# A third copy of q and k in DRAM: stored from SBUF at once, or copied later inside DRAM

## The chip, the cores and the metric

The kernel runs on one core of a Trainium2 chip. The metric is the device time in microseconds (us) of one execution, the median over several runs. The core has a matrix engine (PE, with a separate row PEld for loading weights), a vector engine (DVE), a scalar engine (ACT), a general engine (POOL), and a queue engine (SP) that issues every DMA of this kernel. The DMAs share 16 DMA engines.

## The reference

Attention over a sliding window and a dense GELU block read the same x, and a gate mixes them per row:

```python
def _A_ref(x, wqkv, wo):                 # B, S, D = 1, 2048, 512; H = 32; Dh = 16; W = 256
    qkv = (x @ wqkv).reshape(B, S, 3, H, Dh).transpose(2, 0, 3, 1, 4)
    q, k, v = qkv[0], qkv[1], qkv[2]
    scores = einsum("bhqd,bhkd->bhqk", q, k) * (Dh ** -0.5)
    mask = (idx[:, None] - idx[None, :] >= 0) & (idx[:, None] - idx[None, :] < W)
    p = softmax(where(mask, scores, -1e9))
    o = einsum("bhqk,bhkd->bhqd", p, v)
    return o.transpose(0, 2, 1, 3).reshape(B, S, D) @ wo
def _B_ref(x, w1, b1, w2, b2):           # F = 1792
    return gelu(x @ w1 + b1) @ w2 + b2
g = sigmoid((x * gate_w).sum(-1, keepdims=True))
return g * _A_ref(...) + (1 - g) * _B_ref(...)
```

Everything is float32.

## The kernel before

The matrix products are made of three passes over numbers that are split into a high part (rounded) and a low part (the rest): high times high, high times low, low times high. Lines 127, 128 and 129 (`mm3`) are these three passes.

The 2048 rows of x are cut into four tiles of 512 rows (t = 0 to 3). The PE's main stream is written by a generator, `dense`: first `qkv` for the four tiles (stage "qk", the first 146 us of the trace), then eight turns of the dense block (`mlp`, each with a stage "u" for the first product and a stage "y" for the second), then the output product (`final`). The attention is woven into that stream by the main loop over u. Its 32 heads form eight groups g of four heads, and each group has 16 key blocks of 128 rows, so u runs over 128 steps, with a lead of 12 steps for the pass that finds the row maxima (`att_max`, PE line 541, tile sm). The scores proper are `att_exp` (PE line 585, tile st, exponential on ACT in line 607), and the product with v is `att_pvs` (line 629).

q and k pass through DRAM. `qkv_qk` computes, for one tile t, 128 of q's columns (j = 0 to 3) or of k's (j = 4 to 7), and `qk_out` splits the result into a high and a low part, tile `qke`, and stores it into SQ[t] or SK[t]. There each row of a head has three slots: two for the two parts, and a third that repeats the high part, so that one matrix product over 48 rows of a head covers all three passes. The store is two DMAs: line 348 writes the two parts (512 KB) and line 349 writes the repeated part (256 KB), from the same tile in SBUF. Over the whole kernel these are 32 DMAs of each kind. Index i, the number of the 128 columns, runs from 0 to 3; the groups g = 0 to 3 read i = 0 and 1, the groups 4 to 7 read i = 2 and 3.

The loads for the attention are `load_kd` (line 509) and `load_qd` (lines 501, 496, 498) for the maxima, `load_ks` (the same three lines, tile ks) and `load_qs` (line 520) for the scores; `att_load_v` (line 526) brings v. In one group each of them comes once for every tile t. Their buffers have two slots, so a load waits until the PE has done with the block before the last.

The order of all instructions on PE, DVE, ACT, POOL and SP is written out when the kernel is built: `after` puts a step on a list with a due time in an assumed time, `tick` lets that time pass, and `need` draws a step forward when its result is wanted. On the chip, each engine goes through its own order, and an instruction that waits holds up all behind it. This holds for SP too. Its DMAs take eight completion counters in turn, so that a DMA is issued only when the one eight places before it has landed.

Weights of the dense block come through `load_now` (line 189, tile raw_w), are rounded by ACT (`split`, line 197, tile w) and completed by DVE (line 201).

Of the kernel before, what the change touches and what calls it, by code (L numbers as in the profile page):

```python
# [9 lines left out]
F32 = mybir.dt.float32  # L10
# [7 lines left out]
S, D, F, H, DH, W = 2048, 512, 1792, 32, 16, 256  # L18
T = 512
NT = S // T  # L20
NB = T // 128
NC = D // 128
# [10 lines left out]
def gated_mix(ctx: ExitStack, tc: tile.TileContext, x, wqkv, wo, w1, b1, w2, b2, gate_w, out):  # L33
    nc = tc.nc
# [6 lines left out]
    dr = ctx.enter_context(tc.tile_pool(name="dr", bufs=1, space=DRAM))  # L41
# [4 lines left out]
    def f32(ap):  # L46
        return ap.bitcast(F32)
# [9 lines left out]
    nc.gpsimd.memset(idle, 0.0)  # L57


    SQ = [dr.tile([H // NC, 16, 3, NC, T], F32, name=f"SQ{t}") for t in range(NT)]  # L60
    SK = [dr.tile([H // NC, 16, 3, NC, T], F32, name=f"SK{t}") for t in range(NT)]
    SV = [dr.tile([128, NB, 2, H // 2 * 17], F32, name=f"SV{t}") for t in range(NT)]
    XT = [dr.tile([NC, 128, 2, T], F32, name=f"XT{t}") for t in range(NT)]
    OT = [dr.tile([NC, 128, T], F32, name=f"OT{t}") for t in range(NT)]
# [47 lines left out]
    def halves(v):  # L112

        return v.rearrange("p (a c) -> p a c", a=2)
# [17 lines left out]
    now, todo, done = [0.0, 0], [], set()  # L132

    def after(ns, fn, *args):
        now[1] += 1
        heapq.heappush(todo, (now[0] + ns, now[1], fn, args))

    def step_todo():
        due, _, fn, args = heapq.heappop(todo)
        keep, now[0] = now[0], due  # L140
        fn(*args)
        now[0] = max(keep, due)

    def tick(ns):
        now[0] += ns
        while todo and todo[0][0] <= now[0]:
            step_todo()

    def need(*keys):
        for key in keys:  # L150
            while key not in done:
                step_todo()
# [103 lines left out]
        v = qd[:, i // 2, i % 2]  # L256
        nc.scalar.activation(v, nil.broadcast_to([128, 2 * T]), AF.Copy)

    xts, xrs = {}, {}

    def load_xr(t, bs=range(NB)):
        for b in bs:
# [69 lines left out]

    def qk_out(t, j, p):

        dst, i = (SQ[t], j) if j < NC else (SK[t], j - NC)
        e = sb.tile([128, 2, T], F32R, tag="h", bufs=7, name=f"qke{t}_{j}")

        h = 1 if j < NC else 0

        def hi():  # L340
            nc.scalar.activation(halves(e[:, h]), p, AF.Copy)  # L341

        def lo():
            nc.vector.tensor_sub(halves(e[:, 1 - h]), p, halves(f32(e[:, h])))  # L344

        def store():
            to = dst[:, :, :, i].rearrange("h d s c -> (h d) s c")
            nc.sync.dma_start(to[:, 0:2], f32(e))
            nc.sync.dma_start(to[:, 2], f32(e[:, h]))
            done.add(("qk", t, j))  # L350
        after(100, hi), after(700, lo), after(700 + HOLDQ, store)

# [109 lines left out]
                gate(t + 1)  # L462


    vts, Ms, pts = {}, {}, {}

    def slot(g_, c):
        return (g_ * NT + c) % 2

    def heads(st, g_):  # L470

        return st[2 * (g_ % 4):2 * (g_ % 4) + 2, :, :, 2 * (g_ // 4):2 * (g_ // 4) + 2]

    def ready(t, g_, k):
        need(*[("qk", t, k * NC + 2 * (g_ // 4) + a) for a in range(2)])

    def part(st, g_, s):

        return heads(st, g_)[s].rearrange("d u a c -> (d u) (a c)")

    def load_ks(g_, c):


        ready(c, g_, 1)
        n = 2 * NB
        put_pairs([f32(ks[64 * s + 4:64 * s + 52, slot(g_, c)]) for s in range(2)], SK[c], g_)

    def put_pairs(to, st, g_):

        n = 2 * NB  # L490
        for s in range(2):
            v = to[s].rearrange("r a x -> r (a x)")
            src = part(st, g_, s)
            if s:
                mid = v[:, 192:192 + 256 * (n - 1)].rearrange("r (n x) -> r n x", x=256)[:, :, 0:128]
                nc.sync.dma_start(mid, src[:, 64:64 + 128 * (n - 1)].rearrange("r (n x) -> r n x", x=128))
                ends = v.rearrange("r (n j) -> r n j", j=64)[:, 0:4 * n:4 * n - 1]
                nc.sync.dma_start(ends, src.rearrange("r (n j) -> r n j", j=64)[:, 0:2 * n:2 * n - 1])
            else:
                v = v.rearrange("r (n x) -> r n x", x=256)[:, :, 64:192]  # L500
                nc.sync.dma_start(v, src.rearrange("r (n x) -> r n x", x=128))

    def load_kd(g_, c):
        for t in range(max(c - 1, 0), c + 1):
            ready(t, g_, 1)
            k0 = 0 if t == c else T - W
            at = W if t == c else 0
            src = heads(SK[t], g_)[:, :, :, :, k0:].rearrange("s d u a c -> (s d u) a c")
            nc.sync.dma_start(f32(kd[0:96, slot(g_, c), :, at:at + T - k0]), src)

    def load_qd(g_, c):
        ready(c, g_, 0)
        put_pairs([f32(qd[48 * s:48 * s + 48, slot(g_, c)]) for s in range(2)], SQ[c], g_)

    def load_qs(g_, c):
        ready(c, g_, 0)
        need(("v", NT - 2, NB - 1))
        for s in range(2):
            v = f32(qs[64 * s + 4:64 * s + 52, :, c * T:(c + 1) * T])
            nc.sync.dma_start(v, part(SQ[c], g_, s).rearrange("r (a c) -> r a c", a=2))  # L520

    def att_load_v(g_, c):
        need(*[("v", c, b) for b in range(NB)])
        vt = vbuf[:, c % 2]
        dst = vt[:, 0:NB * 68].rearrange("p (j c) -> p j c", c=34)
        nc.sync.dma_start(dst, SV[c].rearrange("p j s c -> p (j s) c")[:, :, 34 * g_:34 * g_ + 34])
        vts[g_, c] = vt

    def att_max(g_, b, i):

        if b % RB == 0 and (g_, b // RB) not in Ms:
            Ms[g_, b // RB] = sb.tile([128, 2 * RB, 2], F32, tag="M", bufs=2, name=f"M{g_}_{b}")
        M = Ms[g_, b // RB]
        hb, pr = divmod(i, 2)
        c, n = b // NB, slot(g_, b // NB)
        j = 2 * (b % NB) + hb
        w = min(64 * (2 * b + hb + 1), W + 64)
        k1 = 64 * (j + 1) + W
        p = ps.tile([128, 320], F32, tag="sm", bufs=3, name=f"sm{g_}_{b}_{i}")
        v = pairs(p[:, :w])  # L540
        nc.tensor.matmul(v, qd[0:96, n, pr, 128 * j:128 * (j + 1)], two(kd[0:96, n, pr, k1 - w:k1]),  # L541
                         start=True, stop=True)

        def red():
            nc.vector.tensor_tensor_reduce(v, v, two(mask[:, 320 - w:320]), 1.0, -3e38,  # L545
                                           ALU.add, ALU.max, M[:, 2 * (b % RB) + hb, pr:pr + 1])
            done.add(("max", g_, b, i))
        tick(w / 2.4 + 13)
        after(100, red)
# [399 lines left out]
    def fill(ns):  # L949

        owed[0] += ns
        while owed[0] > 0:
            c = next(run)
            if c is None:
                owed[0] = -1e9
            else:
                owed[0] -= c
                tick(c)
# [7 lines left out]
    for u in range(-LEAD, NU):  # L966
        m = u + LEAD
        gm, bm = divmod(m, NKB)
        step = STEP if u >= 0 else STEP0
        for i in range(4):  # L970
            if i == 1 and m % NB == 0 and NB <= m < NU - NB:
                load_kd(*divmod(m // NB + 1, NT)), load_qd(*divmod(m // NB + 1, NT))
            if i % 2 == 0:
                pair = (i, i + 1) if stage[0] != "u" else (i,)
            elif len(pair) == 2:
                continue
            else:
                pair = (i,)
            for op, i in [(op, k) for k in pair for op in ORDER[:3]] + [("f", k) for k in pair]:
                if op == "s" and u >= 0:  # L980
                    att_exp(u // NKB, u % NKB, i)
                if op == "m" and m < NU:
                    att_max(gm, bm, i ^ XOR)
                if op == "p" and i == PVAT and 1 <= u <= NU - LEAD:
                    att_pvs(u - 1)
                if op == "f":
                    fill(step / 4)
        if m < NU and bm % RB == RB - 1:
            after(900, att_rows, gm, bm // RB)
        if m % NB == QAT % NB and QAT <= m < QAT + NKB:  # L990
            load_qs(0, (m - QAT) // NB)
        if u > NU - LEAD:
            att_pvs(u - 1)
        if u % NB == 0 and NB <= u < NU - NB:
            load_ks(*divmod(u // NB + 1, NT))
        if u % NB == 2 and NB < u < NU - 3 * NB:
            load_qs(*divmod(u // NB + 3, NT))
        if u % NB == 0 and u >= 0:
            att_load_v(*divmod(u // NB, NT))
        if u - NU + NKB == YAT:  # L1000
            for k in range(6):
                after(1500 + YGAP * k, load_y, *divmod(k, 2))
    for n, c in enumerate(run):
        tick(c or 0)
        if n == HELD:
            att_pvs(NU - 1)
# [33 lines left out]
AHEAD = 9e3  # L1040
STEP0 = 2750.0
PVAT = 2
HELD = 2
YAT = 5
YGAP = 2500
# [21 lines left out]
```

## Time and profile before

| what | value |
|---|---|
| time, median of 3 runs | 717.82 us (714.51 to 720.12) |
| the profiled execution's own time | 720.44 us |
| its span, first to last instruction | 718.6 us |
| mean granted clock of the PE | 0.994 |
| PE busy | 696.9 us (97% of the span) |
| DVE busy | 514.2 us (72%) |
| ACT busy | 420.0 us (58%) |
| POOL busy | 363.5 us (51%) |
| DMA | 172.09 MB, mean 239 GB/s |
| stores of the repeated part, line 349 | 32 of 256 KB |

The views give times in us from the span's start. In a view of windows the engines stand with the time they were busy in the window and the number of instructions, then the PE's granted clock as a share of full speed, the mean busy share of the DMA engines (it can come out a little above 1) and the rate at which they moved data. In a timeline a row has its start, its length, engine, line and operation, and in brackets the idle time before it and what ended it. A row of SPq is the issue of a DMA; the transfer itself comes after. In the chain of waits a DMA's piece reaches from its issue to its landing. Lines "A <- B: 5.1, 8, 1.0" say that A waited for B for 5.1 us in all, 8 times, at most 1.0 us.

### The profile page before, as it was taken

Reading aid. Unit: us, or ns where it says so; the run is one execution under the profiler, and the core shown is the slowest. Engines: PE = TensorE matmul, PEld = TensorE weight load, DVE = VectorE, ACT = ScalarE, POOL = GpSimd, SP = SyncE. Lnnn points to the kernel's source line nnn. Section 1 sums busy time; section 2 is a strip of 40 time slices with the busy share of each in tenths; the row PEclk is TensorE's granted clock in tenths of the full one; section 3 lists DMA queues with packets and bytes.
Section 4 is the critical chain, followed back from the end, with each engine's and each line's share of the span. In section 5 each row is a group of like instructions: output and inputs, shape, how many; then the busy total and the mean of one; then the engine's idle time right before and its main releaser. Section 6 shows DMA issues by size and latency. Waiting matters only on the chain.

```text
span 718.6 us, 17501 instructions
## 1 busy us (share of the span) xinstructions
PE 696.9 (97%) x6129; PEld 599.8 (83%) x6129; DVE 514.2 (72%) x1561; ACT 420.0 (58%) x972; POOL 363.5 (51%) x852
## 2 busy tenths in 40 slices
PE   9999999988999999999999999999999999999998
PEld 7888888776888888888888878888888888868877
DVE  3732425778868977987898789868877986875552
ACT  4434532348546944964696469548845953885451
POOL 4200000548766875786687657757765785620000
PEclk9999999999999999999999999999999999999999
DMA  8989898998998698799776989997799899578573
GB/s 296 355 264 408 286 400 252 286 329 199 276 261 194 149 261 218 192 221 273 187 186 162 243 219 234 236 273 175 187 267 231 211 263 248 137 214 224 191 254 118
DMA packets 179255, 172.09 MB, mean 239 GB/s; under 512 B 56672, under 2 KB 122976, under 8 KB 179168
## 3 DMA queue, kind: packets, MB, share of 16 engines
q1 hardware_dynamic: 179168, 170.97, 85.9%
q8 instruction: 49, 0.80, 0.5%
q14 instruction: 38, 0.31, 0.2%
HBM read 108.53 MB, written 62.39 MB: 238 GB/s over the span
## 4 chain that ended last, share of the span: by engine, by line
PE 76%; DMA 9%; DVE 6%; ACT 6%; issue 1%; SPq 1%; POOL 1%; DVEq 0%; ACTq 0%
PE sm L541 8%; PE st L585 7%; PE pv_sm L629 7%; PE y L127 6%; PE y L129 6%; PE y L128 6%; PE u L127 5%; PE u L129 4%; PE u L128 4%; PE qk L127 3%; PE qk L129 3%; PE qk L128 3%; DMA qd<-SQ 2%; DVE sm L545 2%; DMA raw_w<-in_B_w_dram 2%; PE pv_st L629 2%
## 5 line engine op out<-in xcount | busy, mean ns | idle before, releaser
L545 DVE CUSTOM_DVE_ANT_1 sm<-sm,mask 128x320 f32<-128x320 f32 (+4 forms) x512 | 233.0, 485 | 71.1 <-PE sm L541 66.0
L601 POOL TENSOR_SCALAR_AFFINE_SELECT pt<-pt 64x256 f32<-64x256 f32 (+1 forms) x538 | 215.0, 420 | 102.4 <-ACT pt L607 91.8
L607 ACT ACTIVATE pt<-st 128x320 f32<-128x320 f32 (+4 forms) x512 | 195.4, 422 | 118.2 <-PE st L585 117.4
L541 PE MATMUL sm<-kd,qd 96*128 96x320 f32 (+4 forms) x512 | 148.6, 304 | 8.4 <-DVE M L545 5.1
L585 PE MATMUL st<-qs,ks 128*128 128x320 f32 (+4 forms) x512 | 148.0, 300 | 2.6 <-ACT pt L607 2.5
L567 POOL CAST qs<-tt 4x256 fp32r<-4x256 f32 x256 | 120.2, 470 | 42.7 <-DVE tt L560 31.4
L541 PEld LDWEIGHTS sm<-kd,qd 96*128 96x128 f32 x512 | 97.4, 190 | 28.0 <-DVE M L545 11.7
L585 PEld LDWEIGHTS st<-qs,ks 128*128 128x128 f32 x512 | 98.1, 192 | 14.6 <-ACT pt L607 4.5
L127 PE MATMUL y<-w,h 128*128 128x512 f32 x224 | 85.1, 380 | 0.6 <-DVE sqh L746 0.6
L129 PE MATMUL y<-w,h 128*128 128x512 f32 x224 | 84.9, 379 | 0.0
L128 PE MATMUL y<-w,h 128*128 128x512 f32 x224 | 84.8, 379 | 0.0
L127 PE MATMUL u<-mx,w 128*128 128x512 f32 x196 | 77.4, 395 | 1.2 <-DVE sqh L746 1.2
L129 PE MATMUL u<-mx,w 128*128 128x512 f32 x196 | 74.8, 382 | 0.0
L128 PE MATMUL u<-mx,w 128*128 128x512 f32 x196 | 74.7, 381 | 0.0
L629 PE MATMUL pv_sm<-pt,vbuf 64*32 64x320 f32 (+4 forms) x1408 | 73.2, 346 | 0.2 <-POOL pt L601 0.2
L629 PE MATMUL pv_st<-pt,vbuf 64*32 64x320 f32 (+4 forms) x1408 | 72.9, 346 | 0.0
L545 DVE DVE_READ_ACCUMULATOR2_ANT M<- 128x1 f32 x512 | 71.4, 139 | 0.0
L629 PEld LDWEIGHTS pv_sm<-pt,vbuf 64*32 64x32 f32 x1408 | 49.3, 106 | 20.2 <-issue 2.0
L344 DVE TENSOR_TENSOR qke<-qk,qke 128x512 fp32r<-128x512 f32 x32 | 22.1, 689 | 43.2 <-ACT qke L341 33.9
L341 ACT ACTIVATE qke<-qk 128x512 fp32r<-128x512 f32 x32 | 19.1, 597 | 49.9 <-PE qk L129 34.8
L129 PEld LDWEIGHTS y<-w,h 128*128 128x128 f32 x224 | 42.2, 189 | 6.1
L127 PEld LDWEIGHTS y<-w,h 128*128 128x128 f32 x224 | 42.5, 190 | 3.2 <-DVE sqh L746 0.8
(148 smaller groups left out, 1292.0 us busy)
## 6 DMA issues: line engine op xcount, KB each, us to landing
kd<-SK SPq DMA_DIRECT2D x32, 384.0 KB
qs<-SQ SPq DMA_DIRECT2D x64, 192.0 KB
mx<-XT SPq DMA_DIRECT2D x24, 512.0 KB
SQ<-qke SPq DMA_DIRECT2D x16, 512.0 KB
SK<-qke SPq DMA_DIRECT2D x16, 512.0 KB
ND<-nd SPq DMA_DIRECT2D x32, 256.0 KB
raw_w<-in_B_w_dram SPq DMA_DIRECT2D x28, 256.0 KB
qd<-SQ SPq DMA_DIRECT2D x32, 192.0 KB
```

The source lines that it names most:

```text
L127: nc.tensor.matmul(p, lh, rh, start=first, stop=False)
L128: nc.tensor.matmul(p, lh, rl, start=False, stop=False)
L129: nc.tensor.matmul(p, ll, rh, start=False, stop=last)
L341: nc.scalar.activation(halves(e[:, h]), p, AF.Copy)
L344: nc.vector.tensor_sub(halves(e[:, 1 - h]), p, halves(f32(e[:, h])))
L541: nc.tensor.matmul(v, qd[0:96, n, pr, 128 * j:128 * (j + 1)], two(kd[0:96, n, pr, k1 - w:k1]), start=True, stop=True)
L545: nc.vector.tensor_tensor_reduce(v, v, two(mask[:, 320 - w:320]), 1.0, -3e38, ALU.add, ALU.max, M[:, 2 * (b % RB) + hb, pr:pr + 1])
L567: nc.gpsimd.tensor_copy(dst, src.unsqueeze(1).broadcast_to([4, 2, RB, 32]))
L585: nc.tensor.matmul(pairs(p[:, :w]), ks[:, slot(g_, kb // NB), pr, at:at + 128], two(qs[:, pr, k0:k0 + w]), start=True, stop=True)
L601: nc.gpsimd.affine_select(out=v, in_=v, pattern=[[0, v.shape[1]], [1 - 2 * e, 64]], compare_op=ALU.is_ge, fill=0.0, base=-e, channel_multi ...
L607: nc.scalar.activation(halves(pt[:, hf, pr, :w]), sorted_(p[:, :w]), AF.Exp, scale=SCALE)
L629: nc.tensor.matmul(pv[r // 64][32 * i:32 * i + 32, q - c * T:e - c * T], vts[g_, b // NB][r:r + 64, v:v + 32], rhs(r), start=start, stop=s ...
```

## The change

SQ[t] and SK[t] are each cut into two DRAM tensors, one with i = 0 and 1 and one with i = 2 and 3. For i = 0 and 1 nothing else changes. For i = 2 and 3 `qk_out` stores the two parts as before but not the repeated one. It notes the copy that is to be made, from the slot of the high part to the third slot, in a list `twice`. The main loop takes one copy from the list at each odd u from 17 to 47, and `repeat` issues it as a DMA from DRAM to DRAM on SP. The loads of the groups 4 to 7 need the copy, where they needed the store. There are 16 such copies of 256 KB, in place of 16 of the 32 stores.

```diff
-    SQ = [dr.tile([H // NC, 16, 3, NC, T], F32, name=f"SQ{t}") for t in range(NT)]
-    SK = [dr.tile([H // NC, 16, 3, NC, T], F32, name=f"SK{t}") for t in range(NT)]
+    SQ = [[dr.tile([H // NC, 16, 3, 2, T], F32, name=f"SQ{t}_{i}") for i in range(2)] for t in range(NT)]
+    SK = [[dr.tile([H // NC, 16, 3, 2, T], F32, name=f"SK{t}_{i}") for i in range(2)] for t in range(NT)]
...
     def qk_out(t, j, p):
-        dst, i = (SQ[t], j) if j < NC else (SK[t], j - NC)
+        i = j % NC
+        dst = (SQ, SK)[j // NC][t][i // 2]
...
         def store():
-            to = dst[:, :, :, i].rearrange("h d s c -> (h d) s c")
+            to = dst[:, :, :, i % 2].rearrange("h d s c -> (h d) s c")
             nc.sync.dma_start(to[:, 0:2], f32(e))
-            nc.sync.dma_start(to[:, 2], f32(e[:, h]))
+            if i < 2:
+                nc.sync.dma_start(to[:, 2], f32(e[:, h]))
+            else:
+                twice.append((t, j, to[:, 2], to[:, h]))
             done.add(("qk", t, j))
...
+    def repeat():
+
+        t, j, to, by = twice.pop(0)
+        nc.sync.dma_start(to, by)
+        done.add(("twice", t, j))
...
     def heads(st, g_):
-        return st[2 * (g_ % 4):2 * (g_ % 4) + 2, :, :, 2 * (g_ // 4):2 * (g_ // 4) + 2]
+        return st[g_ // 4][2 * (g_ % 4):2 * (g_ % 4) + 2]
 
     def ready(t, g_, k):
-        need(*[("qk", t, k * NC + 2 * (g_ // 4) + a) for a in range(2)])
+        need(*[(("qk", "twice")[g_ // 4], t, k * NC + 2 * (g_ // 4) + a) for a in range(2)])
...
+        if COPY[0] <= u < COPY[1] and u % 2 == 1 and twice:
+            repeat()
...
+COPY = (17, 49)
```

PE, DVE, ACT and POOL keep the same instructions in the same order. Only SP's order changes, at two kinds of places. The first is where the stores were; this is the last tile (t = 3), around the end of stage qk. In the rows, SQ_82 and SK_86 are tile 3's q and k, qke_2 and qke_6 stand for i = 2, qke_3 and qke_7 for i = 3, and kd and qd are the loads for tile 3 of group 0. SP before:

```order
L189 DMA raw_w_1507<-in_B_w_dram 128x4x128
L348 DMA SQ_82<-qke_2_1502 128x2x512
L349 DMA SQ_82<-qke_2_1502 128x512
L189 DMA raw_w_1507<-in_B_w_dram 128x512
L348 DMA SK_86<-qke_6_1537 128x2x512
L349 DMA SK_86<-qke_6_1537 128x512
L509 DMA kd<-SK_85 96x2x256
L509 DMA kd<-SK_86 96x2x512
L501 DMA qd<-SQ_82 48x8x128
```

SP in the changed kernel, at the same place (line 348 has become 349, 509 is 519 and 501 is 511; SQ_1_86 and SK_1_94 are the second tensors of tile 3, SK_0_93 and SQ_0_85 the first):

```order
L189 DMA raw_w_1503<-in_B_w_dram 128x4x128
L349 DMA SQ_1_86<-qke_2_1498 128x2x512
L189 DMA raw_w_1503<-in_B_w_dram 128x512
L349 DMA SK_1_94<-qke_6_1532 128x2x512
L519 DMA kd<-SK_0_91 96x2x256
L519 DMA kd<-SK_0_93 96x2x512
L511 DMA qd<-SQ_0_85 48x8x128
```

The two stores of the repeated part that stood ahead of the loads kd and qd are gone; everything else stands as it stood. The next two, for i = 3, go in the same way a few rows further on.

The second kind of place is where the copies are. SP before, at u = 17 to 20 (ND is a store of the attention's result, qs and kd and qd are loads of group 1 and 2):

```order
L526 DMA vbuf<-SV_87 128x8x34
L657 DMA ND_0_111<-nd_3_2812 128x512
L520 DMA qs<-SQ_82 48x2x512 x2
L509 DMA kd<-SK_83 96x2x256
L509 DMA kd<-SK_84 96x2x512
L501 DMA qd<-SQ_80 48x8x128
```

SP in the changed kernel (line 472 is the copy; 536, 667, 530 and 519 are the lines 526, 657, 520 and 509 of before):

```order
L536 DMA vbuf<-SV_95 128x8x34
L667 DMA ND_0_119<-nd_3_2804 128x512
L472 DMA SQ_1_80<-SQ_1_80 128x512
L530 DMA qs<-SQ_0_85 48x2x512 x2
L472 DMA SK_1_88<-SK_1_88 128x512
L519 DMA kd<-SK_0_87 96x2x256
L519 DMA kd<-SK_0_89 96x2x512
L511 DMA qd<-SQ_0_81 48x8x128
```

One copy stands ahead of the load qs and one ahead of the loads kd and qd, and so it goes on, two copies for every four steps of u, to the last copy, which stands directly ahead of the first load of group 4.

More of the change, by code (lines that the diff above doesn't have):

```diff
@@ L257, in clear_q @@
         nc.scalar.activation(v, nil.broadcast_to([128, 2 * T]), AF.Copy)
-    xts, xrs = {}, {}
+    xts, xrs, twice = {}, {}, []
     def load_xr(t, bs=range(NB)):
```

## The prediction, made before the changed kernel was run

> **What bounds the kernel now.** I read the page's first part, then who the PE waits for, and then the stretches in which it waits.
>
> ```profile
> PE 696.9 (97%) x6129; PEld 599.8 (83%) x6129; DVE 514.2 (72%) x1561; ACT 420.0 (58%) x972; POOL 363.5 (51%) x852
> PE sm L541 <- DVE M L545: 5.1, 8, 1.0
> PE st L585 <- ACT pt L607: 2.5, 3, 1.5
> PE sm L541 <- DMA qd<-SQ: 2.1, 1, 2.1
> 0.00:140.00 140.00, 137.63 (x692) 120.10 (x693) 63.44 (x161) 57.35 (x143) 23.95 (x60) 1.00 0.94 321
> 140.00:175.00 35.00, 29.14 (x138) 24.45 (x137) 27.83 (x83) 20.56 (x41) 20.78 (x34) 0.95 0.95 262
> 220.00:350.00 130.00, 130.00 (x1333) 113.56 (x1333) 107.65 (x360) 84.94 (x200) 89.73 (x218) 1.00 0.84 212
> ```
>
> The PE is the bound: of a span of 718.6 us it is idle for 718.6 - 696.9 = 21.7 us, and no change to DMAs can win more than that and what the clock loses. The windows (length, busy us of PE, PEld, DVE, ACT, POOL, then clock, DMA share, GB/s) say where. Up to 140 us, the stage in which the stores are made, the PE is idle for only 2.4 us, although the DMA engines are busy to 0.94. From 140 to 175 us, where the attention and the first turn of the dense block begin, it is idle for 35 - 29.14 = 5.9 us, more than a quarter of all its idle time in a twentieth of the span. From 220 to 350 us, where the copies will go, it is not idle at all, and the DMA engines have 16% left.
>
> So two questions decide: how far the DMAs end the waits between 140 and 175 us, and whether the copies fit into 220 to 350 us.
>
> **The place that waits for DMAs.** First the PE's two longest waits there (its timeline), with ACT's row that belongs to the second, then the clock in windows of 5 us, then the chain of waits in this stretch, then SP's issues of the four stores that go.
>
> ```profile
> 157.42 0.37 PE L541 MATMUL sm<-kd,qd 96*128 96x320 f32 x1 [2.13 <-DMA qd<-SQ]
> 171.70 0.40 PE L585 MATMUL st<-qs,ks 128*128 128x320 f32 x1 [1.51 <-ACT pt L607]
> 170.69 0.63 ACT L197 ACTIVATE w<-raw_w 128x512 fp32r<-128x512 f32 x1 [2.03 <-DMA raw_w<-in_B_w_dram]
> 155.00:160.00 5.00, 2.87 (x11) 2.34 (x10) 2.62 (x9) 2.01 (x5) 1.27 (x1) 0.77 1.04 365
> 160.00:165.00 5.00, 5.00 (x26) 4.46 (x25) 4.84 (x15) 4.75 (x11) 3.22 (x7) 0.89 1.02 274
> 165.00:170.00 5.00, 5.00 (x29) 4.47 (x27) 4.24 (x13) 3.62 (x9) 4.61 (x9) 1.00 1.15 204
> 170.00:175.00 5.00, 2.62 (x12) 1.59 (x11) 3.65 (x7) 4.09 (x9) 4.70 (x8) 1.00 0.58 144
> ```
>
> ```profile
> 149.27 7.59 DMA qd<-SQ
> ...
> 157.36 6.04 DMA SK<-qke
> 163.41 0.02 issue
> 163.42 7.24 DMA raw_w<-in_B_w_dram
> 170.67 0.02 issue
> 170.69 0.64 ACT w L197
> 171.33 0.02 issue
> 171.35 1.74 DVE w L201
> ```
>
> ```profile
> 144.12 0.47 SPq L349 DMA_DIRECT2D SQ<-qke  x1
> 146.70 0.54 SPq L349 DMA_DIRECT2D SK<-qke  x1
> 153.57 0.33 SPq L349 DMA_DIRECT2D SQ<-qke  x1
> 157.36 0.47 SPq L349 DMA_DIRECT2D SK<-qke  x1
> ```
>
> The first wait, 2.13 us, ends with the load qd of tile 3, which was issued at 149.27 and took 7.59 us, in a stretch where the DMA engines' share stands at 1.04. Two of the stores that go were issued 5.2 and 2.6 us before it. Right after this wait the granted clock falls (0.77 and 0.89 in the two windows), which costs 0.23 x 5 + 0.11 x 5 = 1.7 us of PE time. The second wait, 1.51 us, is put down to ACT, but ACT itself had stood for 2.03 us for a weight, raw_w, with the exponential behind it in its queue. The chain shows why that weight was late: it was issued at 163.42, as soon as the store SK<-qke that SP had issued at 157.36 had landed, and this is one of the four stores that go (SP lets only eight DMAs be under way). Both waits hang on one stream of DMAs that is full from 145 to 170 us; at 170 to 175 us its share falls to 0.58, so the backlog is gone there.
>
> **What the removal is worth.** The price of a store comes from the stretch that is made of such stores and little else (87 to 103 us), a row of the view of DMAs:
>
> ```profile
> DMA packets 2933, 6.37 MB, mean 398 GB/s; under 512 B 244, under 2 KB 436, under 8 KB 2932
> ```
>
> 262,144 bytes at 398 GB/s are 0.66 us of all engines. At the mean rate of 140 to 175 us, 262 GB/s (windows above), it would be 1.0 us. I take 0.66, since that row is of the same operation. Step by step:
>
> 1. Twelve of the 16 stores belong to tiles 0 to 2, before 103 us. They free 12 x 0.66 = 7.9 us of DMA time, but the PE idles 2.4 us in all before 140 us, and these rows say for what:
>
> ```profile
> PE warm0.0_180 L386 <- POOL idle L57: 1.2, 1, 1.2
> PE xp L280 <- DMA xr<-in_A_x_dram: 0.4, 1, 0.4
> 132.02 0.48 PE L127 MATMUL qk<-xt,qk 128*128 128x512 f32 x1 [0.76 <-ACT vx L370]
> ```
>
>    The first two are the start, ahead of any store; the third (a row of the PE's timeline) is at 132 us in tile 3, 30 us after the last of the twelve. I count 0.
>
> 2. The first wait: two stores fewer ahead of qd bring it 2 x 0.66 = 1.3 us earlier. The wait shrinks from 2.1 to 0.8 us, and I expect the clock to stay up after it, as it did after the 1.51 us at 171.70 (clock 1.00 in that window). That brings the PE 1.3 + 1.7 = 3.0 us ahead.
>
> 3. The second wait takes part of this back. Four stores fewer bring raw_w 4 x 0.66 = 2.6 us earlier, so ACT, and with it the PE, goes on at 171.70 - 2.6 = 169.1. The PE, 3.0 us early, arrives at 170.19 - 3.0 = 167.2 and waits 1.9 us instead of 1.5. What is left of both steps is 2.6 us: the gain is that of the DMA stream, not the sum of the waits.
>
> 4. After 175 us every engine keeps its order, the PE is the bound, and a lead of 2.6 us stays to the end.
>
> The tile qke is also free a little earlier, and SP has the same number of DMAs to issue in all. Both at 0.
>
> The Trainium skill, "TensorE: Matmul & The Clock Gate" (Part 1 and "HAM oscillation"), says that the clock halves after about one idle window of 3.4 us, and that the window runs freely. Here it fell after 2.13 us idle, so the measured gap decides against the length, and the free window makes it a matter of chance which of two gaps of 1.5 to 2 us is hit. By the page's length, neither gap would cost the clock anything.
>
> **What the copies cost.** They are issued between these rows of SP: the first behind the store ND, the second ahead of the pair of kd loads, the last (row of 349.04) ahead of group 4.
>
> ```profile
> 230.16 0.34 SPq L657 DMA_DIRECT2D ND<-nd  x1
> 232.78 7.05 SPq L509 DMA_DIRECT2D kd<-SK  x2
> 349.04 0.32 SPq L509 DMA_DIRECT2D kd<-SK  x1
> SPq L509 <- PE st L585: 14.8, 10, 6.5
> DMA packets 179255, 172.09 MB, mean 239 GB/s; under 512 B 56672, under 2 KB 122976, under 8 KB 179168
> 320.00:330.00 10.00, 10.00 (x139) 8.61 (x139) 7.64 (x25) 4.29 (x11) 6.59 (x16) 1.00 1.00 227
> ```
>
> No transfer inside DRAM is in the trace. The lower bound is the store, 0.66 us. For the upper one I take reading and writing one after the other at the rate of the fullest window of that stretch (227 GB/s at a share of 1.00): 2 x 262,144 bytes / 227 GB/s = 2.3 us. I take 1.0 us, nearer the store: the rows are as long (2 KB) and the write is the same. That makes 16 x 1.0 = 16 us (10.6 to 37 us) against a free share of 0.16 x 130 = 20.8 us. Spread out two for every four steps of u, the copies raise the share from 0.84 to about 0.96.
>
> What hides them is SP's lead. Between 215 and 345 us SP stands for 14.8 us just until the PE has freed a slot of kd (the row with L509), once 6.5 us long; a copy ahead of such a wait costs nothing. The tightest load that I find is that of ks for the last tile of group 2:
>
> ```profile
> 325.52 0.91 SPq L498 DMA_DIRECT2D ks<-SK  x1
> 333.94 0.30 PE L585 MATMUL st<-qs,ks 128*128 128x320 f32 x1
> ```
>
> Its last part is issued at 325.5 and first used at 333.9, 8.4 us later. DMAs in the chain above took 6.0 to 7.6 us, so 0.8 to 2.4 us are to spare, and one copy of 1.0 us stands in the stream ahead of it. If that cover is gone, the PE waits 1 to 2 us, and the clock may cost 1.7 us more. I count 0 for the forecast and keep up to 3.7 us for the range.
>
> **Sum.** 720.4 (the profiled execution) - 2.6 + 0 = 717.8 us. That execution lies 2.6 us above the median of the runs, 717.82, so I forecast 717.8 - 2.6 = 715.2 us.
>
> **Rivals.**
>
> *The clock fall only moves.* If it hits the wait of step 3, 1.7 us go back: gain 0.9 us, 716.9 us. For it: that wait grows to 1.9 us. Against it: the wait of 1.51 us did not trigger it.
>
> *All of the waits go.* If SP, with eight DMAs at most under way, gains more than the bytes say, the 5.9 us of idle PE between 140 and 175 us and 1.7 us of clock are the most that can go: 717.8 - 7.6 = 710.2 us. Against it: the waits on DVE there, part of the 5.1 us above, have another cause.
>
> *One load comes late.* A copy catches a load such as ks with too little to spare: 1 to 2 us of waiting and 1.7 us of clock, less the 2.6 us gained: 717.8 + 3.7 - 2.6 = 718.9 us.
>
> *The copies fill the DMA engines (slower).* Reading and writing DRAM, a copy takes the 2.3 us of the upper bound, 37 us in all against 20.8 us free. The stream falls 16 us behind by 350 us; the spare time of a load takes some 2.4 us of it, and the rest stands before the PE: 717.8 + 16 - 2.4 - 2.6 = 728.8 us. It decides from 20.8 / 16 = 1.3 us a copy on. For it: the full windows (share 1.00 at 320 to 330 us). Against it: that rate comes from loads in short rows (page: of 179,255 packets 122,976 are under 2 KB), and in the stretch of stores, 2,497 of 2,933 of 2 KB or more, it was 398.
>
> The Trainium skill, "DMA: Bandwidth & Descriptors" (Specifications), gives a core about 358 GB/s of DRAM bandwidth; a copy moves its bytes through it twice, which as an estimate by that page is 0.52 MB / 358 GB/s = 1.5 us, on the slow side of that point, and would give 16 x 1.5 = 24 us. The row above with 398 GB/s is already over that figure in one direction; no run here shows both.
>
> *The change does not do what it says:* the loads of groups 0 to 3 could stay behind the copies. The order of SP above excludes it, since copies and these loads touch different tensors.
>
> **Chances.** Forecast 0.50 (own range 713.5 to 716.5), the clock moves 0.18, all waits go 0.10, one load late 0.14, engines full 0.08. About 1%, 7.2 us, is what a measurement of this kernel can tell from no change; the three runs before lie 5.6 us apart. Faster by over 1% is half of "all waits go" and some scatter of the forecast: 0.08. Slower by over 1% is most of the last case: 0.07. Within 1%: 0.85. The range leaves out the far ends of "all waits go" and "engines full": 711 to 720 us.
>
> **What would show it.** Right: the wait of sm on qd near 157 us falls to about 0.8 us, the clock rows 0.77 and 0.89 go, raw_w near 170 us comes 2.6 us earlier, and 220 to 350 us keeps a fully busy PE with a DMA share of about 0.96. Wrong: PE waits on kd, qd, ks or qs after 220 us, a copy that takes over 1.3 us of the engines, or a wait at 157 us as long as before, which would mean that not the stores but SP's issuing or the weights fill the stream.

## The result

The changed kernel takes 715.65 us (median of 13 runs, 711.05 to 719.60) against 720.12 us (median of 13 runs, 714.51 to 725.96) for the kernel before. The ratio is 0.9937, with a 95% interval of 0.9913 to 0.9962: faster by 0.6%, or 4.5 us (2.7 to 6.3). A second comparison of the same two kernels gave 0.9921 (0.9887 to 0.9954).

The profiled execution of the changed kernel took 713.22 us, with a span of 711.4 us. Its page, and then its windows (length, busy us of PE, PEld, DVE, ACT, POOL, then clock, DMA share, GB/s):

```profile
PE 694.0 (98%) x6129; PEld 596.5 (84%) x6129; DVE 511.6 (72%) x1561; ACT 419.6 (59%) x972; POOL 365.2 (51%) x852
```

```profile
0.00:140.00 140.00, 138.47 (x703) 121.20 (x704) 64.96 (x170) 58.36 (x145) 25.57 (x61) 1.00 0.91 307
140.00:175.00 35.00, 33.19 (x225) 26.92 (x224) 31.74 (x98) 25.89 (x55) 25.71 (x46) 1.00 1.01 266
220.00:350.00 130.00, 130.00 (x1371) 113.15 (x1350) 108.07 (x358) 84.91 (x197) 92.51 (x221) 1.00 0.95 247
```

Between 140 and 175 us the PE is now idle for 1.8 us, where it was idle for 5.9 us, and its clock does not fall. (The windows are the same times, not the same work: the changed kernel is some us further on in each.) Between 220 and 350 us it is still busy all of the time, while the DMA share went from 0.84 to 0.95. The waits of the PE from 128 to 180 us, first of the kernel before, then of the changed one:

```profile
PE sm L541 <- DVE M L545: 2.1, 3, 0.9
PE sm L541 <- DMA qd<-SQ: 2.1, 1, 2.1
PE st L585 <- ACT pt L607: 1.5, 1, 1.5
PE qk L127 <- ACT vx L370: 0.8, 1, 0.8
PE sm L541 <- DMA SV<-vx: 0.5, 1, 0.5
```

```profile
PE sm L551 <- DVE M L555: 1.9, 4, 1.0
PE pv_sm L639 <- POOL pt L611: 0.7, 1, 0.7
PE pv_st L639 <- POOL pt L611: 0.2, 1, 0.2
```

The wait on qd is gone altogether, not shrunk to 0.8 us, and so are the wait on ACT's exponential and the two short ones of 0.8 and 0.5 us that come before 142 us. Since the order on the PE is the same in both kernels, the two traces can be laid side by side, matmul by matmul. The changed kernel is ahead by 1.2 us after the start, by 4.1 us at the first product of stage u (142.50 against 146.59 us), by 8.1 us behind the old wait on qd and the slow clock after it (153.16 against 161.29 us), and by 7.7 us at the first product of stage y (174.48 against 182.21 us). About 6.5 us were won between 130 and 180 us, of which 1.7 us are the fall of the clock that is gone. Outside of this stretch, 1.2 us is the start, and 2.2 us near 427 us go with a second fall of the clock in the profile of before, which three of the other profiles show there too (tiles 0 to 2, tiles 0 and 1, and small stores kept, below) and the rest do not, whatever the stores do. The profiled executions lie 7.2 us apart; the medians lie 4.5 us apart.

That the clock falls in one execution and not in another is seen in the other executions as well. Each has its mean granted clock on record: 0.9971 to 0.9976 on average in the four sets of runs of the kernel before (17 to 32 runs each), 0.9992 and 0.9993 in the two sets of the changed one (13 and 7 runs). As an estimate, a clock short by 0.0024 over 718 us is 1.7 us, and one short by 0.0008 is 0.6 us, so about 1.1 us of the gain is clock on average.

The traffic of the copies shows in the page's third part, first before, then after:

```profile
HBM read 108.53 MB, written 62.39 MB: 238 GB/s over the span
```

```profile
HBM read 112.73 MB, written 62.39 MB: 246 GB/s over the span
```

4.2 MB are read more, and as much is written as before: 16 copies of 262,144 bytes in place of 16 stores.

### The profile page after: what moved, and what is told of

Same layout as the page of the kernel before. It is cut to its first block, busy times and chain, and to the rows that moved or that the text cites. A ratio compares the mean times of both kernels' runs of the same rounds, so it can differ in the third digit from the quotient of the medians.

```text
span 711.4 us, 17481 instructions
## 1 busy us (share of the span) xinstructions
PE 694.0 (98%) x6129; PEld 596.5 (84%) x6129; DVE 511.6 (72%) x1561; ACT 419.6 (59%) x972; POOL 365.2 (51%) x852
## 3 DMA queue, kind: packets, MB, share of 16 engines
q1 hardware_dynamic: 179168, 170.97, 87.4%
## 4 chain that ended last, share of the span: by engine, by line
PE 77%; DVE 8%; ACT 5%; DMA 5%; POOL 3%; issue 1%; SPq 0%; DVEq 0%; ACTq 0%; POOLq 0%
PE sm L551 8%; PE pv_sm L639 7%; PE st L595 7%; PE y L127 6%; PE y L129 6%; PE y L128 6%; PE u L127 4%; PE qk L127 4%; PE u L129 4%; PE qk L129 4%; PE u L128 4%; PE qk L128 4%; DVE sm L555 3%; PE v L127 2%; PE v L129 2%; PE v L128 2%
## 5 line engine op out<-in xcount | busy, mean ns | idle before, releaser
L129 PEld LDWEIGHTS y<-w,h 128*128 128x128 f32 x224 | 42.2, 189 | 6.1
L660 ACT ACTIVATE nd<-pv_st 128x512 f32<-128x512 f32 x32 | 19.1, 597 | 45.2 <-PE pv_sm L639 39.4
```

Source lines behind the costliest of these rows:

```text
L129: nc.tensor.matmul(p, ll, rh, start=False, stop=last)
```

## The experiments

Each edit is made in the changed kernel; the ratios are to the kernel before on the same chip, with 95% intervals. In each edit `t` is the tile and NT - 1 is tile 3; where a kernel stores at once what the changed kernel copies, its later loads wait for the store.

### One tile, or the other three

Tile 3 alone, which holds the four stores on which the prediction rests:

```diff
-            if i < 2:
+            if i < 2 or t < NT - 1:
```

> Only the four stores of tile 3 (i = 2 and 3) become later copies; the twelve of tiles 0 to 2 are stored at once as before. Prediction's account (only the stores directly ahead of the late loads count, by their bytes): all of the gain, ratio to before 0.994, about 715.7 us. Rival account (SP issues without a gap from 89 to 139 us, so a store removed in tile 2 moves everything behind it): the three short PE waits between 130 and 147 us stay, the wait on qd near 157 us shrinks by about 1.3 us, ratio 0.996 to 0.998, about 718 us.

Measured: 717.62 us, ratio 0.9975 (0.9938 to 1.0011). The time is not told apart from no change, nor from the 2.6 us of the prediction. The PE's waits between 128 us and stage u (which begins at 146.98 us here) are these rows of its timeline:

```profile
132.47 0.48 PE L127 MATMUL qk<-xt,qk 128*128 128x512 f32 x1 [1.21 <-ACT vx L374]
141.79 0.55 PE L551 MATMUL sm<-kd,qd 96*128 96x320 f32 x2 [0.55 <-DMA qd<-SQ]
146.09 0.40 PE L551 MATMUL sm<-kd,qd 96*128 96x320 f32 x1 [0.73 <-DVE M L555]
```

The wait on a qd that is left here, 0.55 us, is not the one of the prediction: it is on tile 2's load, issued at 136 us. The wait near 157 us on tile 3's load is gone altogether, where 0.8 us was forecast, and so is that on ACT's exponential near 171 us, where 1.9 us was forecast. What stayed are the waits before stage u, 2.5 us together against 2.1 us in the kernel before.

The twelve stores of tiles 0 to 2 alone:

```diff
-            if i < 2:
+            if i < 2 or t == NT - 1:
```

> The twelve stores of tiles 0 to 2 (i = 2 and 3) become later copies; the four of tile 3 are stored at once as before. Prediction's account: no gain, ratio 1.000, 720 us. Rival account: the loads kd and qd of tile 2 are issued about 4 us earlier (at about 129 us less what the start differs), the three short PE waits between 130 and 147 us (2.1 us together in the profile before) go, and the PE reaches the first product of the dense block 2 to 3 us earlier; ratio 0.995 to 0.997, 716.5 to 718.5 us.

Measured: 713.60 us, ratio 0.9918 (0.9885 to 0.9951). The stores that were counted at nothing bring the gain without tile 3's. The waits on ACT and on SV before 142 us are gone; the wait on tile 3's qd is left with 1.3 us, and that on the exponential with 0.9 us.

```profile
PE sm L551 <- DMA qd<-SQ: 1.3, 1, 1.3
PE sm L551 <- DVE M L555: 1.2, 3, 0.5
PE st L595 <- ACT pt L617: 0.9, 1, 0.9
```

How stores that have landed by 109 us (the last is issued at 102.5) come to matter at 132 us is seen in SP's timeline. First the kernel before, the end of tile 2:

```profile
95.23 1.08 SPq L349 DMA_DIRECT2D SQ<-qke  x1
96.36 1.30 SPq L424 DMA_DIRECT2D XT<-qs  x1
97.76 0.54 SPq L348 DMA_DIRECT2D SK<-qke  x1
98.35 1.08 SPq L349 DMA_DIRECT2D SK<-qke  x1
99.53 1.07 SPq L348 DMA_DIRECT2D SQ<-qke  x1
100.64 0.84 SPq L349 DMA_DIRECT2D SQ<-qke  x1
101.58 0.90 SPq L348 DMA_DIRECT2D SK<-qke  x1
102.52 0.84 SPq L349 DMA_DIRECT2D SK<-qke  x1
103.46 0.91 SPq L501 DMA_DIRECT2D qd<-SQ  x1
```

Then the changed kernel at the same place (line 349 is now the store of the two parts):

```profile
91.68 1.12 SPq L428 DMA_DIRECT2D XT<-qs  x1
92.90 1.00 SPq L349 DMA_DIRECT2D SK<-qke  x1
94.00 1.06 SPq L349 DMA_DIRECT2D SQ<-qke  x1
96.63 0.36 SPq L349 DMA_DIRECT2D SK<-qke  x1
97.08 1.04 SPq L511 DMA_DIRECT2D qd<-SQ  x1
```

How far SP is behind its work shows in the last qke of tile 2, which DVE completes in these rows, before and after:

```profile
97.14 0.69 DVE L344 TENSOR_TENSOR qke<-qk,qke 128x512 fp32r<-128x512 f32 x1 [1.64 <-ACT qke L341]
95.91 0.69 DVE L345 TENSOR_TENSOR qke<-qk,qke 128x512 fp32r<-128x512 f32 x1 [1.63 <-ACT qke L342]
```

In the kernel before, it is done at 97.8 us and its store is issued at 101.58 us, 3.7 us later. One issue follows the other without a gap, and each takes 0.5 to 1.3 us while the DMA engines' share is 1.04 (90 to 105 us); at 81 us, in a stretch with a share of 0.81, the same two lines took 0.38 and 0.46 us. In the changed kernel the tile is done at 96.6 us and stored at 96.63 us: SP has a gap at 95 us, has caught up and waits for that tile. From there SP is the carrier. Before, it stops only between 106.8 and 110.0 us, four times for 0.3 to 0.7 us, each time until an earlier DMA has landed (the changed kernel stops at the same rows), and then has no gap of over 0.3 us up to 128.7 us, in a stretch of many small DMAs. From 110 to 120 us the engines' share is 0.85, so it seems to be SP's issuing that sets the pace there; no run shows that apart. What SP is behind at 103 us it is still behind at 129: the changed kernel issues the same row 6.4 us earlier at 103 us, 5.2 us at 118 us (the first weight of the dense block, 118.54 against 113.38 us) and 5.9 us at 129 us, of which 1.2 us are the start. ACT rounds these weights with the result of v behind them in its queue, and waits for them from 95 to 147 us as follows, before and after:

```profile
ACT w L197 <- DMA raw_w<-in_B_w_dram: 12.4, 5, 3.2
```

```profile
ACT w L197 <- DMA raw_w<-in_B_w_dram: 0.3, 1, 0.3
```

ACT stands longer for other things in the changed kernel (5.7 us for POOL instead of 1.8), but from 128 to 180 us no wait of the PE is on ACT any more.

### The cut in two alone

```diff
-            if i < 2:
+            if True:
```

> SQ and SK are cut in two, but all 32 repeated parts are stored at once and no copy is made. All accounts that rest on the stores: as before, ratio 1.000, PE waits between 130 and 175 us as before. If the shorter row pitch in DRAM were the cause: ratio 0.994.

Measured: 719.92 us, ratio 0.9998 (0.9964 to 1.0032), with PE busy for 29.43 of the 35 us from 140 to 175 us (before 29.14). Where the rows lie in DRAM is not the cause. Its profile serves as a second one of the kernel before, and it shows one thing more: the wait on tile 3's qd is 1.0 us there, not 2.1, and the clock did not fall.

```profile
155.00:160.00 5.00, 3.97 (x23) 3.38 (x22) 4.19 (x15) 3.17 (x7) 2.36 (x3) 1.00 1.05 400
160.00:165.00 5.00, 4.60 (x25) 3.83 (x23) 4.99 (x15) 4.93 (x12) 3.59 (x8) 1.00 1.08 275
```

The kernel with tiles 0 and 1 alone copied later, further down, has the wait as long as before. Its clock stayed up behind it and fell at 171 us, after waits of 1.74 and 0.74 us:

```profile
155.36 0.37 PE L551 MATMUL sm<-kd,qd 96*128 96x320 f32 x1 [2.06 <-DMA qd<-SQ]
155.00:160.00 5.00, 4.64 (x26) 4.32 (x27) 4.09 (x12) 4.07 (x9) 2.42 (x3) 1.00 0.98 338
170.00:175.00 5.00, 4.26 (x14) 3.14 (x13) 5.00 (x14) 4.91 (x12) 4.23 (x10) 0.66 0.44 123
```

### Bytes or issues

At the place of each store that is gone, a store of its first 16 columns is put back:

```diff
             else:
+                nc.sync.dma_start(to[:, 2, 0:16], f32(e[:, h, 0:16]))
                 twice.append((t, j, to[:, 2], to[:, h]))
```

> As the changed kernel, but at the place of each of the 16 removed stores a store of the first 16 columns is issued (8 KB, 128 rows of 64 bytes): the same number of DMAs on SP as before in the stage qk, with 4 MB less to move there. If the bytes on the DMA engines set the pace: as the changed kernel, ratio 0.994. If SP's time for one issue and its limit of eight DMAs under way set it: as before, ratio 1.000, with the PE waits between 130 and 160 us back.

Measured: 714.99 us, ratio 0.9937 (0.9904 to 0.9971), as the changed kernel. For the time it is the bytes that count and not the number of DMAs. For SP itself the number is not free: the first qd is issued about half way between the kernel before and the changed one (table below), but that part of the delay reaches the PE nowhere before stage u.

### Which tile

Tile 2 alone, tiles 0 and 1 alone, and later all but tile 2, and tiles 2 and 3:

```diff
-            if i < 2:
+            if i < 2 or t != 2:      # tile 2 alone
+            if i < 2 or t >= 2:      # tiles 0 and 1 alone
+            if i < 2 or t == 2:      # all but tile 2
+            if i < 2 or t < 2:       # tiles 2 and 3
```

> Only tile 2's four stores (i = 2 and 3) become later copies. Theory now: in the profile before, SP has gaps at 74.6 and 75.5 us and then none over 0.3 us until 106.8 us; so what the stores of tiles 0 and 1 delay is made up by 75 us, and the bytes of tile 2's four stores make the delay that lasts to 139 us. Then the load of qd for tile 0 is issued 4 us earlier than before (91 to 93 us after the first qk product, against 96.5), and nearly all of the gain of the twelve is there: ratio 0.991 to 0.995. Rival (every store counts alike): a third of it, 0.997, and qd earlier by 1.8 us.

> Only the eight stores of tiles 0 and 1 (i = 2 and 3) become later copies. Theory now: SP's gaps around 75 us grow, the load of qd for tile 0 is issued as before (about 96 us after the first qk product), ratio 0.998 to 1.000. Rival (every store counts alike): two thirds of the gain of the twelve, 0.994 to 0.995, and qd earlier by 3.6 us.

> The changed kernel with one part undone: tile 2's four stores are made at once again, the other twelve stay later copies. Theory now (tile 2's bytes make the delay that SP carries to 139 us): little is left of the gain, ratio 0.997 to 1.000; qd for tile 0 is issued at 95 to 97 us after the first qk product and the PE's first product of stage u comes at 138.5 to 140.5 us after it (before 139.7, changed kernel 136.5). Prediction's account (tile 3's stores count): the gain stays, 0.994.

> Only the eight stores of tiles 2 and 3 become later copies; those of tiles 0 and 1 are made at once. Theory now: the same as the changed kernel up to 200 us (qd for tile 0 at 91 to 93 us, first product of stage u at 136 to 137 us after the first qk product), with half of the copies and a DMA share of about 0.90 instead of 0.95 from 220 to 350 us; ratio 0.992 to 0.995, not to be told from the changed kernel. If the stores of tiles 0 and 1 matter by themselves: 0.996 to 0.998.

> The changed kernel itself, beside the next one on the same chip: ratio to before 0.991 to 0.996.

> Only tiles 2 and 3 become later copies, again, to compare with the changed kernel on the same chip. If the eight copies less between 220 and 350 us are worth something in time, it is faster than the changed kernel by 1 to 3 us, as the first pass hinted (0.9899 against 0.9937); if what SP had to spare there hid all 16 copies and that pass was scatter, both give the same time within 1 us. If the stores of tiles 0 and 1 matter by themselves, it is slower by 1 to 2 us.

Measured, with the starts of three rows of the timelines counted from the PE's first product of v (30.55 us in the profile before, 29.32 us in that of the changed kernel). The expectations count from the first qk product, 23 to 24 us earlier; counted so, the first qd is issued at 91.9 us with tile 2 alone (91 to 93 expected), 95.5 with tiles 0 and 1 (96), 94.1 with all but tile 2 (95 to 97) and 92.3 with tiles 2 and 3 (91 to 93). Up to that row of v the profiles differ by up to 1.2 us in the waits of the start; from there on to 128 us the PE does not wait in any of them. Up to 143 us, just ahead of the first u, kernels with the same stores in tiles 0 to 2 have the same order on SP, so what differs among them in the first two columns is scatter: up to 1.9 us for qd, up to 0.9 us for u.

| stores copied later | first qd issued | first u | first y | ratio (95% interval) |
|---|---|---|---|---|
| none (before) | 72.9 | 116.0 | 151.7 | 1 |
| none (cut in two alone) | 71.8 | 116.1 | 149.4 | 0.9998 (0.9964 to 1.0032) |
| tile 3 | 73.6 | 116.9 | 149.8 | 0.9975 (0.9938 to 1.0011) |
| tiles 0, 1 | 71.2 | 114.5 | 150.0 | 0.9974 (0.9947 to 1.0000) |
| tiles 0, 1, 3 | 70.7 | 114.5 | 147.4 | 0.9946 (0.9916 to 0.9976) |
| tile 2 | 68.5 | 113.2 | 145.5 | 0.9960 (0.9928 to 0.9993) |
| tiles 2, 3, twice | 68.9, 69.1 | 113.2, 113.2 | 145.1, 146.0 | 0.9899 (0.9855 to 0.9944), 0.9932 (0.9903 to 0.9961) |
| tiles 0, 1, 2 | 67.8 | 114.0 | 146.8 | 0.9918 (0.9885 to 0.9951) |
| all, small stores kept | 70.3 | 113.2 | 146.0 | 0.9937 (0.9904 to 0.9971) |
| all (changed), twice | 67.8, 68.1 | 113.2, 113.2 | 145.2, 145.4 | 0.9937 (0.9913 to 0.9962), 0.9921 (0.9887 to 0.9954) |

The column of u has a floor. The windows from the first v to the first u say what it is, for the kernel before, the changed one and tile 2 alone:

```profile
30.55:146.59 116.04, 113.94 (x562) 99.59 (x560) 52.25 (x150) 44.32 (x120) 14.37 (x33) 1.00 0.94 319
29.32:142.50 113.18, 113.18 (x561) 99.73 (x560) 50.75 (x150) 44.32 (x120) 14.36 (x33) 1.00 0.90 306
30.42:143.60 113.18, 113.18 (x561) 99.72 (x559) 50.72 (x150) 44.41 (x120) 14.33 (x33) 1.00 0.93 321
```

At 113.2 us the PE works without a pause (the one row with tile 2 above that, 114.0, has a wait of 0.5 us on DVE). Tile 2's four stores alone take it there, as all 16 do, and bring it to stage y as early (145.5 against 145.2 and 145.4 us). But the theory that they are the only cause fell. The eight stores of tiles 0 and 1, whose delay was expected to be made up by 75 us, bring 1.6 of the 2.9 us up to u by themselves; and without tile 2's, the other twelve bring more than half of the gain at the first y (147.4, against 149.4 and 151.7 with none), and a ratio of 0.9946, where 0.997 to 1.000 was expected. Up to u, then, the parts do not add up (1.6 and 2.9 us alone, 2.9 us at most together): the backlog has to be shortened by enough, for which the four stores of tile 2 do more than the eight of tiles 0 and 1, and when the waits are gone, more is worth nothing. From u to y the same is likely, since tile 3 alone and tiles 0 and 1 alone stand with the kernels without copies there and the twelve together do not, but that rests on one profile per row. The ratios could not tell it: their intervals are as wide as the differences among the parts.

Tiles 2 and 3 together looked better than the changed kernel in the first comparison. Side by side on one chip they took 714.97 and 714.49 us, so the first look was scatter, and half of the copies do as well as all, and not measurably better.

### More copies

The copy is issued twice, or four times, the further ones into DRAM tensors that nothing reads (a list `spill`, made beside SQ and SK):

```diff
         nc.sync.dma_start(to, by)
+        for _ in range(1):       # 3 for four times
+            nc.sync.dma_start(spill.pop(), by)
```

> As the changed kernel, but each of the 16 copies is issued twice, the second time into a DRAM tensor that nothing reads: 4 MB more read and written between 220 and 350 us. If the copies lie beside the PE's work with room to spare: the time of the changed kernel, 715.7 us, PE busy all of the time from 220 to 350 us, DMA share about 1.0 there. If the room is used up by the first 16 (share 0.95): the 16 further copies of 0.9 us of the engines each exceed it by 8 us, loads of ks come late, 2 to 8 us slower than the changed kernel.

> As the changed kernel, but each copy is issued four times, three of them into DRAM tensors that nothing reads: 48 further copies of 0.9 us of the engines, 43 us, against 7 us that are free between 220 and 350 us. If a copy costs the engines 0.9 us: at least 20 us slower than the changed kernel, with PE waits on kd, qd or ks. If copies inside DRAM run beside the other transfers almost without cost: the time of the changed kernel.

Measured: doubled 720.45 us, ratio 1.0038 (0.9999 to 1.0076); fourfold 744.00 us, ratio 1.0360 (1.0309 to 1.0412). Against the changed kernel's 0.9937 that is some 7 us and some 30 us more. The profile of the doubled copies is of an execution of 726.65 us, 6 us above the median, so its waits are longer than in most. The windows from 220 to 350 us, then the waits of the PE, and of DVE on DMAs, from about there (to 360 us) with the copies doubled:

```profile
220.00:350.00 130.00, 124.70 (x1296) 107.16 (x1295) 101.48 (x341) 80.25 (x187) 86.26 (x211) 1.00 0.97 258
```

```profile
PE sm L554 <- DVE M L558: 4.3, 4, 2.3
PE st L598 <- DMA ks<-SK: 1.0, 1, 1.0
```

```profile
DVE num L696 <- DMA rb<-RD: 5.4, 3, 3.2
DVE yo L846 <- DMA YA<-yo: 4.3, 1, 4.3
```

and with the copies fourfold, the same window, in which the clock falls too:

```profile
220.00:350.00 130.00, 118.40 (x1134) 101.17 (x1120) 92.48 (x306) 74.00 (x170) 78.06 (x190) 0.93 0.98 272
```

The load ks that the prediction named does come late, but it costs 1.0 us. More comes by a way that it did not name: DVE stands for a transfer of the attention's normalization (rb) and for an old store of the dense block (YA), with the row maxima behind it in its queue, and the PE waits for those. DVE's wait on YA in this stretch is a first sign of it even where the PE loses nothing: 0.6 us before, 1.3 us in the changed kernel, 4.3 us doubled.

## Why the prediction was right, and where not

**Time and range.** Forecast 715.2 us, range 711 to 720; measured 715.65. Within 1% had 0.85, and so it is. That the time comes so close is in part luck: the forecast gain of 2.6 us was too small (4.5 us, 2.7 to 6.3), and the median of three runs from which it was taken, 717.82 us, lay 2.3 us below the median of 13.

**What bounds the kernel.** Right. The PE is the bound, and the gain is idle time between 130 and 180 us, with about 1 us of clock.

**Step 1, twelve stores at 0: this step failed.** It went by the PE's waits before 140 us and by their distance in time from the stores, and did not follow what carries a delay from one to the other. The twelve alone give a ratio of 0.9918. SP, behind by the bytes of the stores, did not catch up until after 128 us; the rows that would have shown it are SP's timeline, which has no gap from 89 to 106 us, the 3.7 us between a tile's last row on DVE and its store, and ACT's waits on raw_w, 12.4 us from 95 to 147 us in the profile before.

**Step 2, the wait on qd.** Right in place; the size was not met. With tile 3 alone the wait is gone, where 0.8 us was forecast to be left, and the PE comes to stage u 0.9 us later there, which hides a part of it. One profile does not settle the price of two stores, 1.3 us: with all of tile 3's stores in place the same wait was 2.1, 1.0, 2.1 and 1.3 us in four profiles (before, cut in two alone, tiles 0 and 1, tiles 0 to 2), and none in a fifth (tile 2). The 1.7 us of clock were counted as sure and are not: of the two waits of 2.1 us, one was followed by a fall at once and one was not. On average over the executions about 1.1 us of clock did come back, at whatever places.

**Step 3, the second wait.** Its forecast failed: the wait on the exponential was to grow to 1.9 us, and it is gone, with tile 3 alone and in the changed kernel. A later wait does take part of the lead back, but it is another one: the changed kernel is 9.4 us ahead at the product of st ahead of the first products with v (168.68 against 178.12 us) and 7.7 us at the first y. In those products it now waits for POOL's pt (0.7 and 0.2 us in the rows of the result); the rest of these 1.7 us is not taken apart. The 2.6 us for tile 3 alone are not confirmed either: 0.9975 is 1.8 us, with an interval that takes in 0 and 2.6, and the first y of that profile (149.8) lies between those of the two without copies.

**Step 4, the lead stays.** Right: from 200 to 350 us the distance between the traces is 7.7 to 7.8 us throughout.

**The copies.** Right in price and in effect: the share rose by 0.11 over 130 us, which is 14.3 us or 0.9 us of the engines a copy (1.0 forecast, 0.66 to 2.3 as bounds), and the PE lost nothing. That share is good to some 0.04, or 0.3 us a copy, since the two profiles of tiles 2 and 3 have 0.94 and 0.90 there, where 0.90 was expected. The 48 further copies of the fourfold kernel give a second figure: the page has the queue's packets at 88.6% of 739.9 us there and at 87.4% of 711.4 us in the changed kernel, 33.8 us more or 0.7 us a copy. What hides them seems to be SP's lead, and most of it is used up: SP's wait for a slot of kd between 220 and 350 us, before and after, is

```profile
SPq L509 <- PE st L585: 18.5, 11, 6.5
```

```profile
SPq L519 <- PE st L595: 6.6, 5, 5.3
```

**The rivals.** "The copies fill the DMA engines" was right in kind, from a price of 1.3 us a copy on; at 0.9 us the 16 stay below it, and 32 lie above it and are slower by 7 us. "One load comes late" is what ks shows there. "All of the waits go" came closer than its chance of 0.10 said: the PE's idle time from 140 to 175 us fell by 4.1 of 5.9 us. SP does gain more than the four stores' bytes say, but by the bytes of the other twelve, which the rival did not name. The tensors were cut so that the loads of groups 0 to 3 do not touch the copies, and nothing in the trace contradicts it.

**The price of a copy, and the clock.** The Trainium skill, "DMA: Bandwidth & Descriptors" (Specifications), gives about 358 GB/s of DRAM bandwidth for a core, from which the estimate was 1.5 us a copy; measured are 0.7 to 0.9 us of the engines, so the trace decides against that estimate. The Trainium skill, "TensorE: Matmul & The Clock Gate" (Part 1), has the window run freely; a fall of the clock behind a wait of 2.13 us in one profile and none behind one of 2.06 us at the same place in another fits that.

## What to carry to other kernels

A queue that issues without a gap carries a delay further than the transfers that made it, here from 103 to 129 us: before a transfer is counted at nothing because it is long over, follow the issuing queue to its next gap, and read who waits for what stands behind it. Moving bytes out of a full stretch pays up to the point where the waits are gone, so a part of the move can be worth as much as the whole, and a part alone little. Where moved work is hidden, doubling it shows how much room is left and which engine feels it first.

## What was not expected of the hardware

A copy inside DRAM took no more of the DMA engines than 0.7 to 0.9 us for 256 KB, some 290 to 370 GB/s, although each byte is read and written there; the stretch of stores from SBUF ran at 398 GB/s. The clock of the PE fell to half behind an idle time of 2.13 us in one profile (for 3.4 us, 157.7 to 161.1), but not behind 2.06 us at the same place in another, nor behind the longest wait of the changed kernel's profile, 2.41 us at 681 us.
